# Lag tables built with half-scale squares and fewer complex products, in a newly ordered S4 convolution and GLU kernel

## The chip, the cores and the metric

The kernel runs on one core of one Trainium2 chip. The metric is the device time of one execution in microseconds (us); several executions are timed and their median is given. Engines are named as in the profile: PE is the matrix engine (PEld its weight loads), DVE the vector engine, ACT the scalar engine, POOL the GpSimd engine, SP the engine that issues most DMAs.

## The reference

The input is normalized by a layernorm, and two independent branches read the result; everything is bfloat16 at the edges.

```python
def _A_ref(u, A_re, A_im, B_re, B_im, C_re, C_im, log_dt, Dskip):   # u: [1, 2048, 512], A..C: [512, 128]
    dt = jnp.exp(log_dt)[:, None]
    logdA = dt * (A_re + 1j * A_im)
    dB = dt * (B_re + 1j * B_im)
    P = jnp.exp(logdA[:, :, None] * l[None, None, :])               # l = 0 .. 2047
    K = jnp.einsum("dn,dnl,dn->dl", C_re + 1j * C_im, P, dB).real    # one kernel of 2048 taps per channel
    ...                                                             # y = causal convolution of u with K, by rfft of length 4096
    return y + u * Dskip[None, None, :]

def _B_ref(x, w_gate, w_up, w_down):                                # 512 -> 1792 -> 512
    h = _sigmoid(x @ w_gate) * (x @ w_up)
    return h @ w_down

xn = _layernorm(x)
return x + _A_ref(xn, ...) + _B_ref(xn, ...)
```

## The kernel before

**Work of the two branches.** The GLU branch goes over four groups of 512 rows. For each group and each of 14 slices of the hidden width it runs four gate matmuls (line 1021), a sigmoid on ACT (1030), four up matmuls (1036) and a product on DVE (1051); then four sets of 14 down matmuls (1069). The product reads the up result either straight from its PSUM bank, or from an SBUF copy (`us_sb`) that ACT made (1047); the set `UEV` lists the units that take the copy.

The convolution branch never forms a long FFT. It transforms the input by matmuls with small constant matrices (691, through a DRAM scratch `z_scr`, then 891), multiplies it with the spectrum of K (products on DVE, lines 915 and 919), transforms back (932, through the scratch `v_scr`) and finishes with matmuls at line 989. The spectrum of K comes from matmuls with constant weights E (909), eight units for each half of the channels. The first 8 of the 16 products can run when half of the channels has its K, the last 8 need the other half.

**The lag tables.** K at the lag l is a sum over 128 modes of a power of a complex number. The power is split into two tables, G (16 steps of 16 lags, with C and dB in it) and H (41 base lags, listed in `LAG0`), and K is a matmul of the two (818). The tables are made in four parts of 128 channels each (loop variable `c`); all four use one buffer H, so a part may write H only when the matmuls of the part before have read it. Inside a part, new lags come from old ones in two ways. A *product* (`cmul`, called by `powers` for `n` lags at a time) multiplies by a constant power W: two wide DVE multiplies (729, 730), then a subtract and an add (734, 735). A *square* (`squares`) doubles the exponent: ACT squares real and imaginary parts in place (784), and DVE makes the real part by a subtract (789), the imaginary part by a product (790), and doubles it (791). The W come from a ladder of 11 repeated squarings in float32 (ACT 668, DVE 674 and 676, copies to bfloat16 on ACT 662).

**The start.** While weights arrive, DVE and ACT compute the layernorm statistics of each 128-row tile (`ON_ACT` lists the tiles that ACT takes), and the phase of the discretized A: DVE reduces it modulo one turn (619 to 621), ACT takes exponentials and sines (623 to 628), DVE combines them (635 to 637). Until real work is there, PE runs dummy matmuls on zeros (526).

**The order.** Nothing is scheduled at run time. All pieces of work are recorded as numbered operations with dependencies, and the table `ORDER` is the order in which they are written out; each engine executes its own instructions in just that order and waits on semaphores. Buffers are taken and given back in the same order.

Of the kernel before, what the change touches and what calls it, by code (L numbers as in the profile page):

```python
# [20 lines left out]
D = 512  # L21
# [33 lines left out]
LAG0 = (list(range(16)) + [256 + 2 * j for j in range(8)] + [512 + 4 * j for j in range(4)] + [768 + 4 * j for j in range(4)]  # L55
        + [1024, 1032, 1280, 1288, 1536, 1792, 1544, 1800, 2048])
# [104 lines left out]
def _build_E(S1, M2):  # L161

    E = np.zeros((NKT, 8, NGE, NU, 128))
    z = M2.reshape(NU, 2, 2, 32, 128)
    s1 = S1.reshape(32, NU, 2, 2)
    for l in range(L):
        h, i = _row(l)
        if h < 40 and (h < 32) == (l < 1024):
            E[h // 8, h % 8, i] += np.einsum("gpc,gpcf->gf", s1[l % 1024 // 32], z[:, :, :, l % 32, :])
    E = E.reshape(NKT, 128, NU, 128).transpose(1, 2, 0, 3)  # L170
    E[:, 1::2] = np.roll(E[:, 1::2], 64, axis=-1)
    return E

def _consts():
# [134 lines left out]
def kernel(  # L309
# [83 lines left out]
    for nm, sz in [("W1", 12 * KB), ("gc", 2 * KB), ("G", 16 * KB), ("H", 20992), ("tmp", 4 * KB), ("W0", 12 * KB),  # L393
                   ("xn", 16 * KB), ("lad", 16 * KB), ("kx", 8 * KB), ("zs", 4 * KB), ("pq", 2 * KB)]:
        OFF[nm] = o
        o += sz
    KQ = o
    W = [at(OFF["W%d" % p], [12, 2, DW]) for p in range(NP)]
    gc = at(OFF["gc"], [2, D])
    xn = at(OFF["xn"], [NT, D])  # L400

# [52 lines left out]
    for n in range(3):  # L454
# [3 lines left out]
        if n == 1:  # L458
            l_s1 = load("SP", s1[:], cten["S1"].ap(), 64 * KB)
# [680 lines left out]
```

## Time and profile before

| what | value |
|---|---|
| time before, median of 3 runs | 254.12 us (253.22 to 255.28) |
| the profiled execution's own time | 252.33 us |
| span of its instructions, first to last | 250.5 us |
| granted PE clock, mean | 0.986 |
| PE busy | 222.8 us (89%) |
| DVE busy | 202.0 us (81%) |
| ACT busy | 184.3 us (74%) |

The span is 1.8 us shorter than the execution's own time, and that execution is 1.8 us faster than the median of the timed runs. Matmuls are pipelined and the end of each is modelled, so the busy time of PE includes some waiting; how many matmuls of a kind start in a stretch says more. DVE instructions overlap at their ends as well: the distance from one start to the next is what an instruction costs there, and it is a little shorter than its duration.

### The profile page before, as it was taken

The numbers are of one execution on the slowest core, as the hardware profiler recorded it, in microseconds if no ns is written. First come the engines' busy times: TensorE is split into PE (matmuls) and PEld (weight loads), VectorE is DVE, ScalarE is ACT, GpSimd is POOL, SyncE is SP. The second block draws the span as 40 slices with busy tenths as digits, with TensorE's granted clock in tenths as the row PEclk, the third lists the DMA queues.
The fourth block names the chain that finished last, engine by engine and source line by source line (L and its number), as shares of the span: only waits on it lengthen the run. The fifth ranks groups of instructions, "written<-read, shape, count | busy, mean of one in ns | idle before, by whom it ended". The sixth has DMA issues, their size and how long they took to land.

```text
span 250.5 us, 5787 instructions
## 1 busy us (share of the span) xinstructions
PE 222.8 (89%) x2246; PEld 120.0 (48%) x2276; DVE 202.0 (81%) x445; ACT 184.3 (74%) x297; POOL 15.5 (6%) x34
## 2 busy tenths in 40 slices
PE   0799999999996799599999799979799999999994
PEld 0264444444432544246555556434565555544762
DVE  2999999999999999999999999999435244672652
ACT  5799999999998989358998698877446589740000
POOL 2202600010000000000000040000001010000000
PEclk9999999999999999979999799999999999999999
DMA  6999946305262585236737977734557698679263
GB/s 156 257 346 359 351 146 124 99 3 126 84 168 85 167 219 133 77 91 184 200 71 198 268 119 190 231 93 143 138 180 205 185 243 243 161 210 304 91 196 128
DMA packets 50861, 43.64 MB, mean 174 GB/s; under 512 B 12561, under 2 KB 44050, under 8 KB 50834
## 3 DMA queue, kind: packets, MB, share of 16 engines
q1 hardware_dynamic: 48738, 40.58, 55.8%
q0 software_dynamic: 864, 1.57, 3.9%
q10 hardware_dynamic: 1232, 1.11, 1.4%
q8 instruction: 18, 0.29, 0.5%
q14 instruction: 9, 0.07, 0.1%
HBM read 24.64 MB, written 12.06 MB: 147 GB/s over the span
## 4 chain that ended last, share of the span: by engine, by line
DVE 45%; PE 34%; ACT 11%; issue 6%; DMA 3%; DVEq 0%; ACTq 0%
PE bank L1021 8%; DVE big L729 8%; DVE big L730 8%; PE bank L1069 7%; DVE big L735 6%; DVE big L734 5%; PE bank L1036 5%; DVE hT_sb L1051 4%; PE pair L909 4%; DVE big L915 3%; ACT big L662 3%; DVE big L790 3%; PE pair L932 2%; DVE big L789 2%; DVE big L919 2%
## 5 line engine op out<-in xcount | busy, mean ns | idle before, releaser
L1021 PE MATMUL bank<-xnT,wg_sb 128*128 128x512 bf16 (+1 forms) x224 | 54.7, 368 | 3.3 <-ACT us_sb L1047 1.2
L1036 PE MATMUL bank<-xnT,wu_sb 128*128 128x512 bf16 x214 | 54.3, 379 | 3.2 <-DVE hT_sb L1051 1.2
L1069 PE MATMUL bank<-wd_sb,hT_sb 128*128 128x512 bf16 x217 | 52.0, 389 | 1.0 <-ACT glu_sb L1099 0.5
L1021 PEld LDWEIGHTS <-wg_sb 128*128 128x128 bf16 x236 | 22.3, 98 | 27.1 <-issue 5.9
L1030 ACT ACTIVATE hT_sb<-bank 128x512 bf16<-128x512 f32 x56 | 32.2, 598 | 4.1 <-PE bank L1021 4.0
L1069 PEld LDWEIGHTS <-hT_sb 128*128 128x128 bf16 x224 | 21.9, 100 | 27.4 <-issue 4.0
L1036 PEld LDWEIGHTS <-wu_sb 128*128 128x128 bf16 x224 | 20.8, 98 | 28.1 <-issue 5.5
L915 DVE TENSOR_TENSOR big<-big 128x2048 bf16<-128x2048 bf16 x16 | 19.5, 1220 | 14.1 <-DMA big<-big 7.2
L729 DVE TENSOR_TENSOR big<-big 128x512 bf16<-128x512 bf16 (+4 forms) x48 | 27.7, 577 | 1.0 <-ACT big L770 0.2
L730 DVE TENSOR_TENSOR big<-big 128x512 bf16<-128x512 bf16 (+4 forms) x48 | 27.5, 573 | 0.0
L1051 DVE TENSOR_TENSOR hT_sb<-hT_sb,bank 128x512 bf16<-128x512 bf16 x27 | 17.8, 682 | 7.0 <-ACT hT_sb L1030 4.6
L1047 ACT ACTIVATE us_sb<-bank 128x512 bf16<-128x512 f32 x29 | 17.1, 601 | 6.7 <-DVE hT_sb L1051 5.9
L734 DVE TENSOR_TENSOR big<-big 128x256 bf16<-128x256 bf16 (+4 forms) x48 | 20.2, 420 | 0.8
L911 ACT ACTIVATE big<-pair 128x1024 bf16<-128x1024 f32 x16 | 16.5, 1031 | 4.9 <-PE pair L909 3.6
L909 PE MATMUL pair<-big 128*128 128x256 bf16 x160 | 19.8, 273 | 0.3 <-DVE big L853 0.3
L735 DVE TENSOR_TENSOR big<-big 128x256 bf16<-128x256 bf16 (+4 forms) x48 | 20.0, 416 | 0.0
L896 ACT ACTIVATE big<-pair 128x1024 bf16<-128x1024 f32 x16 | 16.3, 1032 | 3.4 <-PE pair L891 3.4
L909 PEld LDWEIGHTS <-big 128*128 128x128 bf16 x160 | 15.3, 98 | 5.0 <-issue 1.5
L693 ACT ACTIVATE big<-pair 128x1024 bf16<-128x1024 f32 x16 | 16.3, 1023 | 1.6 <-PE pair L691 1.6
L936 ACT ACTIVATE big<-pair 128x1024 bf16<-128x1024 f32 x16 | 16.3, 1026 | 1.2 <-PE pair L932 0.4
L691 PE MATMUL pair<-big,s 128*128 128x512 bf16 x31 | 9.7, 394 | 7.9 <-DVE big L559 7.9
L784 ACT ACTIVATE big<-big 128x768 bf16<-128x768 bf16 (+2 forms) x16 | 11.0, 690 | 6.2 <-DVE big L735 6.1
(105 smaller groups left out, 285.2 us busy)
## 6 DMA issues: line engine op xcount, KB each, us to landing
big<-c_E SPq DMA_DIRECT2D x16, 320.0 KB, 3.6
z_scr<-big SPq DMA_DIRECT2D x16, 256.0 KB, 2.7
big<-z_scr SPq DMA_DIRECT2D x16, 256.0 KB, 3.7
big<-big SPq DMA_DIRECT2D x64, 64.0 KB, 3.1
v_scr<-big SPq DMA_DIRECT2D x16, 256.0 KB, 3.7
big<-v_scr SPq DMA_DIRECT2D x12, 256.0 KB, 4.6
big<-in_A_u_dram SPq DMA_DIRECT2D x4, 512.0 KB, 5.8
wu_sb<-in_B_w_up_dram SPq DMA_DIRECT2D x2, 896.0 KB, 6.7
```

Source lines behind the costliest of these rows:

```text
L729: V.tensor_tensor(out=ov, in0=lov, in1=mre, op=ALU.mult)
L730: V.tensor_tensor(out=wide(tb()), in0=lov, in1=mim, op=ALU.mult)
L734: V.tensor_tensor(out=outp[:, :, :, 0, :], in0=outp[:, :, :, 0, :], in1=tb()[:, :, :, 1, :], op=opr)
L735: V.tensor_tensor(out=outp[:, :, :, 1, :], in0=outp[:, :, :, 1, :], in1=tb()[:, :, :, 0, :], op=opi)
L909: T.matmul(two(sk)[:, o:o + DW], es()[:, g, kt, :], kT[p][:, kt, :], start=kt in (0, NKT - 1), stop=kt >= NKT - 2)
L915: V.tensor_tensor(out=pp().rearrange("p q h m -> p (q h) m"), in0=xx().rearrange("p q h m -> p (q h) m"), in1=kb()[:, 0:2 * DW].unsqueeze( ...
L1021: T.matmul(bank(sl)[:, c0:c1], w[:, kt, k * 128:(k + 1) * 128], xnT[:, grp, kt, c0:c1], start=(kt == 0), stop=(kt == KT - 1))
L1030: S.activation(out=hT_sb[:, hs.idx, k % 2, :], in_=bank(sl), func=ACT.Sigmoid)
L1036: T.matmul(bank(sl), wu_sb[:, kt, k * 128:(k + 1) * 128], xnT[:, grp, kt, :], start=(kt == 0), stop=(kt == KT - 1))
L1047: S.activation(out=us_sb[:, us.idx, :], in_=bank(sl), func=ACT.Identity)
L1051: V.tensor_tensor(out=h(), in0=h(), in1=us_sb[:, us.idx, :] if on else bank(sl), op=ALU.mult)
L1069: T.matmul(bank(po), hT_sb[:, hts[k // 2].idx, k % 2, jj * 128:(jj + 1) * 128], wd_sb[:, k, :], start=(k == 0), stop=k == FT - 1, **kw)
```

## The change

- **Squares at half scale.** ACT now squares with the scale 0.5^0.5 into a buffer of its own (`sq_sb`), and the doubling instruction on DVE is gone: what is stored is half of the true power. The constant weights E are multiplied by 2, or by 8 where a square of a square is meant, for the rows listed in `EXP`.
- **Lags in another order.** `LAG0` is rearranged, and a part of H is made by six products and five squares instead of eight products and four squares. The products of 1, 2 and 2 lags at `o0` = 33, 34 and 37 go, one of 4 lags at 33 comes, and a square of one lag (39 from 27) comes.
- **Phase steps on ACT.** The scaling by 1/(2 pi) with the rounding constant becomes one ACT instruction, the two DVE instructions after it do the rest, and 1 - 2 s^2 is one ACT instruction instead of one of DVE.
- **Other moves.** `ON_ACT` is tile 0 alone instead of tiles 1 and 3. `UEV` has 22 units instead of 29. The running sums of `f_pre` go from DVE to POOL. The constants s1, s2, sr and rr lie in space that other tiles use too, so the loads of s2 and sr and the clearing of rr wait for the last table matmul. `ORDER` is another list, and some of the planner's costs, which only served to find that list, are changed.

Lines of the changed kernel are 3 to 7 higher than those of the kernel before. The core of the diff:

```diff
+EXP = {6: 1, 10: 1, 12: 3, 14: 1, 19: 1, 21: 1, 22: 3, 23: 1, 27: 1, 29: 1, 31: 3, 30: 3, 37: 1, 38: 1, 39: 3}
...
-            E[h // 8, h % 8, i] += np.einsum("gpc,gpcf->gf", s1[l % 1024 // 32], z[:, :, :, l % 32, :])
+            E[h // 8, h % 8, i] += 2.0 ** EXP.get(h, 0) * np.einsum("gpc,gpcf->gf", s1[l % 1024 // 32], z[:, :, :, l % 32, :])
...
-UEV = (7, 14, 15, 16, 17, 18, 19, 21, 24, 25, 26, 28, 29, 30, 31, 32, 33, 34, 35, 36, 37, 38, 39, 40, 41, 42, 46, 49, 54)
-ON_ACT = (1, 3)
+UEV = (15, 19, 23, 24, 27, 28, 29, 30, 31, 32, 33, 34, 35, 36, 37, 38, 39, 40, 41, 42, 43, 44)
+ON_ACT = (0,)
 ORDER = [
-    0, 1, 29, 12, 4, 3, 30, 31, 39, 40, 2, 14, 19, 5, 10, 33, 32, 42, 34, 7, 17, 35, 41, 49, 50, 51, 43, 132, 25, 52, 15,
+    1, 0, 38, 28, 27, 37, 3, 4, 47, 2, 30, 29, 48, 50, 31, 49, 39, 52, 41, 51, 32, 14, 5, 7, 17, 10, 18, 6, 40, 34, 12, 42,
...
+    q2b = pl.add("ACT", 0.57, lambda: S.activation(out=pt_["rn"], in_=pt_["z_im"], func=ACT.Identity, scale=INV_2PI, bias=magic[:]), [q1], PR)
     def f_red():
-        V.tensor_scalar(out=pt_["w0"], in0=pt_["z_im"], scalar1=INV_2PI, scalar2=None, op0=ALU.mult)
-        V.tensor_scalar(out=pt_["rn"], in0=pt_["w0"], scalar1=MAGIC, scalar2=MAGIC, op0=ALU.add, op1=ALU.subtract)
-        V.tensor_tensor(out=pt_["w0"], in0=pt_["w0"], in1=pt_["rn"], op=ALU.subtract)
+        V.tensor_scalar(out=pt_["rn"], in0=pt_["rn"], scalar1=MAGIC, scalar2=None, op0=ALU.subtract)
+        V.scalar_tensor_tensor(out=pt_["w0"], in0=pt_["z_im"], scalar=INV_2PI, in1=pt_["rn"], op0=ALU.mult, op1=ALU.subtract)
...
+        S.activation(out=pt_["sh"], in_=pt_["sh"], func=ACT.Identity, scale=-2.0, bias=one[:])
...
-        V.tensor_scalar(out=pt_["sh"], in0=pt_["sh"], scalar1=-2.0, scalar2=1.0, op0=ALU.mult, op1=ALU.add)
...
-        def squares(o0, os, l0, nn, need):
+        def squares(o0, os, l0, ls, nn, need):
...
+            sl = _Slot("sq")
+            a = pl.add("ACT", 0.11 + 0.213 * nn, lambda: S.activation(out=sq().rearrange("p r k c h -> p r k (c h)"), in_=src.rearrange("p r k c h -> p r k (c h)"),
+                                                                      func=ACT.Square, scale=float(0.5 ** 0.5)),
+                       dep(need), PC - 0.5, acq=[sl])
             def f_q():
-                V.tensor_tensor(out=dst[:, :, :, 0, :], in0=dst[:, :, :, 0, :], in1=dst[:, :, :, 1, :], op=ALU.subtract)
+                V.tensor_tensor(out=dst[:, :, :, 0, :], in0=sq()[:, :, :, 0, :], in1=sq()[:, :, :, 1, :], op=ALU.subtract)
                 V.tensor_tensor(out=dst[:, :, :, 1, :], in0=src[:, :, :, 0, :], in1=src[:, :, :, 1, :], op=ALU.mult)
-                V.tensor_scalar(out=dst[:, :, :, 1, :], in0=dst[:, :, :, 1, :], scalar1=2.0, scalar2=None, op0=ALU.mult)
...
         powers(3, 1, 1, 1, 1, 1, [1])
...
-        squares(25, 1, 17, 3, ["17"])
-        powers(28, 1, 16, 2, 4, 9, [16, "17"])
-        powers(34, 1, 16, 4, 2, 10, [16, "17"])
-        squares(36, 2, 28, 2, ["28"])
-        powers(37, 2, 28, 2, 2, 10, ["28"])
-        powers(33, 1, 8, 1, 1, 10, [8])
+        squares(27, 2, 17, 1, 3, ["17"])
+        powers(24, 2, 16, 2, 4, 9, [16, "17"])
+        powers(33, 1, 16, 4, 4, 10, [16, "17", "24"])
+        squares(37, 1, 24, 2, 2, ["24"])
+        squares(39, 1, 27, 1, 1, ["27"])
...
+    l_sr = load("SP", sr, cten["SR"].ap(), 128 * KB, deps=table_free, pkt=1024)
+    l_s2 = load("SP", s2, cten["S2"].ap(), 64 * KB, deps=table_free)
+    m_rr = pl.add("POOL", 0.3, lambda: P.memset(rr, 0.0), table_free, 60)
```

The new order is seen best in the instructions. First, what DVE executes last in the fourth part of the tables. Before (729, 730, 734, 735 are a product, 789 to 791 a square; the last number is the output's shape):

```order
L729 TENSOR_TENSOR big<-big 128x64x8
L730 TENSOR_TENSOR big<-big 128x512
L729 TENSOR_TENSOR big<-big 128x64x2x4
L730 TENSOR_TENSOR big<-big 128x512
L734 TENSOR_TENSOR big<-big 128x64x2x2
L735 TENSOR_TENSOR big<-big 128x64x2x2
L789 TENSOR_TENSOR big<-big 128x64x2x2
L790 TENSOR_TENSOR big<-big 128x64x2x2
L791 TENSOR_SCALAR big<-big 128x64x2x2
```

The same place now, where 733, 734, 738, 739 are a product and 795, 796 a square:

```order
L733 TENSOR_TENSOR big<-big 128x64x16
L734 TENSOR_TENSOR big<-big 128x1024
L795 TENSOR_TENSOR big<-sq_sb 128x64x3x2
L796 TENSOR_TENSOR big<-big 128x64x3x2
L795 TENSOR_TENSOR big<-sq_sb 128x64x2x2
L796 TENSOR_TENSOR big<-big 128x64x2x2
L738 TENSOR_TENSOR big<-big 128x64x4x2
L739 TENSOR_TENSOR big<-big 128x64x4x2
L795 TENSOR_TENSOR big<-sq_sb 128x64x2
L796 TENSOR_TENSOR big<-big 128x64x2
```

Two products of two lags have become one of four, with two squares between its halves, and each square has two instructions in place of three.

Second, the start of PE. Before, it begins with the input transform of a first tile and 14 dummy matmuls (526), and only then come the transposes of the normalized tiles (570):

```order
L691 LDWEIGHTS s_70
L691 MATMUL pair_63<-big,s_70 128x512
...
L526 LDWEIGHTS glu_sb
L526 MATMUL bank_68<-glu_sb 128x512
...
L570 LDWEIGHTS big
L570 MATMUL pair_64<-ident,big 128x128
```

Now the transposes are the first instructions of PE, and the 14 dummies (529) stand behind 56 gate matmuls (1028), right ahead of the first up matmul (1043):

```order
L1028 LDWEIGHTS wg_sb
L1028 MATMUL bank_65<-xnT,wg_sb 128x512
L529 LDWEIGHTS glu_sb
L529 MATMUL bank_68<-glu_sb 128x512
...
L1043 LDWEIGHTS wu_sb
L1043 MATMUL bank_66<-xnT,wu_sb 128x512
```

So the dummies moved from a place where PE had nothing else to do to a place between real matmuls.

Third, ACT at the start, from the exponential of log_dt to the first copy of transposed input (575). Before:

```order
L611 ACTIVATE big<-big 128x512
L693 ACTIVATE big<-pair_63 128x1024
L623 ACTIVATE big<-big 128x512
L626 ACT_TABLE_LOAD
L626 ACTIVATE big<-big 128x512
L627 ACTIVATE big<-big 128x512
L628 ACTIVATE big<-big 128x512
L575 ACTIVATE xnT<-pair_64 128x4x256
```

Now, with the two added steps at 621 and 633:

```order
L614 ACTIVATE big<-big 128x512
L621 ACTIVATE big<-big,magic 128x512
L627 ACTIVATE big<-big 128x512
L630 ACT_TABLE_LOAD
L630 ACTIVATE big<-big 128x512
L631 ACTIVATE big<-big 128x512
L632 ACTIVATE big<-big 128x512
L633 ACTIVATE big<-big,one 128x512
L578 ACTIVATE xnT<-pair_63 128x4x256
```

The evacuation of a transformed tile (693) has left this place, and two short steps of the phase have come into it, one of them right ahead of the first copy of transposed input.

More of the change, by code (lines that the diff above doesn't have):

```diff
@@ L352 @@
     ident = const.tile([128, 128], BF, name="ident")
-    s1 = const.tile([128, 2, 128], BF, name="s1")
-    s2 = const.tile([128, 2, 128], BF, name="s2")
     dskr = const.tile([1, D], BF, name="dskr")
@@ L357 @@
     rz = const.tile([128, KT, 8], BF, name="rz")
-    rr = const.tile([128, D], BF, name="rr")
-    sr = const.tile([128, 4, 128], BF, name="sr")
+    sq_sb = const.tile([128, 2, NPR * 12], BF, name="sq_sb")
     wg_sb = const.tile([128, KT, F], BF, name="wg_sb")
@@ L458 @@
         if n == 1:
-            l_s1 = load("SP", s1[:], cten["S1"].ap(), 64 * KB)
+            l_s1 = load("SP", s1, cten["S1"].ap(), 64 * KB)
         if n:
@@ L499, in fw_ @@
                 V.tensor_copy(out=q["m_f"], in_=q["m_b"])
-            o_v = pl.add("DVE", 0.37, fv_, deps, prio)
+            o_v = pl.add("DVE", 0.8 if t1 - t0 > 1 else 0.37, fv_, deps, prio)
             o_w = pl.add("DVE", 0.22, fw_, deps, prio)
@@ L516 @@
     half = const.tile([128, NT], BF, name="half")
+    magic = const.tile([128, 1], F32, name="magic")
+    one = const.tile([128, 1], F32, name="one")
     P.memset(half[:], 0.5)
+    P.memset(magic[:], MAGIC)
+    P.memset(one[:], 1.0)
     P.memset(glu_sb[:, 0, :], 0.0)
     P.memset(rz[:], 0.0)
-    P.memset(rr[:], 0.0)
     wsl = _Slot("po")
@@ L628, in f_sin @@
         S.activation(out=pt_["sh"], in_=pt_["sh"], func=ACT.Square)
-    q5 = pl.add("ACT", 1.6, f_sin, [q3, q4], PR, tab="sin")
+        S.activation(out=pt_["sh"], in_=pt_["sh"], func=ACT.Identity, scale=-2.0, bias=one[:])
+    q5 = pl.add("ACT", 2.15, f_sin, [q3, q4], PR, tab="sin")
     lad0 = OFF["lad"]
@@ L634, in f_w0 @@
     def f_w0():
[L635 removed]
         V.tensor_tensor(out=wt[0][:, 0, :], in0=pt_["rr"], in1=pt_["sh"], op=ALU.mult)
         V.tensor_tensor(out=wt[0][:, 1, :], in0=pt_["rr"], in1=pt_["sn"], op=ALU.mult)
[L638 removed]
+    cur_op = pl.add("DVE", 1.25, f_w0, [q5], PR)
     def f_g():
@@ L642, in f_g @@
         tt(perm(pt_["db_im"]), raw("B", 1), perm(dtb), ALU.mult)
-    qb = pl.add("DVE", 2.0, f_g, [o_dt] + pt_op["B"], PR + 2)
+    qb = pl.add("DVE", 1.21, f_g, [o_dt] + pt_op["B"], PR + 2)
     def f_g2():
@@ L648, in f_g2 @@
         tt(gc[:, 0, :], pt_["t1"], pt_["t2"], ALU.subtract)
-    qc1 = pl.add("DVE", 1.9, f_g2, [qb] + pt_op["C"], PR + 2)
+    qc1 = pl.add("DVE", 2.02, f_g2, [qb] + pt_op["C"], PR + 2)
     def f_g3():
@@ L701, in f_pre @@
     def f_pre():
-        V.tensor_copy(out=pre[:, :, 0], in_=xnT[:, 0, :, 0])
+        P.tensor_copy(out=pre[:, :, 0], in_=xnT[:, 0, :, 0])
         for t in range(1, 4):
-            V.tensor_tensor(out=pre[:, :, t], in0=pre[:, :, t - 1], in1=xnT[:, 0, :, 128 * t], op=ALU.add)
-        V.tensor_copy(out=pre2[:, :, 0], in_=xnT[:, 0, :, 64])
-        V.tensor_tensor(out=pre2[:, :, 1], in0=pre2[:, :, 0], in1=xnT[:, 0, :, 192], op=ALU.add)
-    o_pre = pl.add("DVE", 1.0, f_pre, xnT_ready[0], 47)
+            P.tensor_tensor(out=pre[:, :, t], in0=pre[:, :, t - 1], in1=xnT[:, 0, :, 128 * t], op=ALU.add)
+        P.tensor_copy(out=pre2[:, :, 0], in_=xnT[:, 0, :, 64])
+        P.tensor_tensor(out=pre2[:, :, 1], in0=pre2[:, :, 0], in1=xnT[:, 0, :, 192], op=ALU.add)
+    o_pre = pl.add("POOL", 2.0, f_pre, xnT_ready[0], 47)
     kq = at(KQ, [NHP, 16])
@@ L736, in cmul @@
         a = pl.add("DVE", 0.14 + 0.27 * n, f_a, deps, prio, acq=[sl])
-        return pl.add("DVE", {1: 0.37, 2: 0.45, 3: 0.62, 4: 0.70}.get(n, 0.15 + 0.134 * n), f_b, [a], prio - 0.1, rel=[sl])
+        return pl.add("DVE", {1: 0.37, 2: 0.48, 4: 0.73, 7: 1.19}.get(n, 0.15 + 0.134 * n), f_b, [a], prio - 0.1, rel=[sl])
     kgen = {}
@@ L792, in squares @@
-            h_ops[str(o0)] = pl.add("DVE", 0.18 + 0.185 * nn, f_q, [a], PC - 0.5)
+            h_ops[str(o0)] = pl.add("DVE", 0.22 + 0.134 * nn, f_q, [a] + hdep, PC - 0.5, rel=[sl])
         powers(3, 1, 1, 1, 1, 1, [1])
-        squares(6, 1, 3, 1, ["3"])
+        squares(6, 1, 3, 1, 1, ["3"])
         powers(5, 2, 1, 2, 2, 2, [1, "3"])
         powers(9, 2, 1, 2, 4, 3, [1, "3", "5"])
-        squares(10, 2, 5, 3, ["5", "6"])
+        squares(10, 2, 5, 1, 3, ["5", "6"])
         powers(17, 1, 2, 2, 7, 8, [2, 4, 8, "6", "10"])
-        squares(25, 1, 17, 3, ["17"])
@@ L961, in f_rz @@
         V.tensor_tensor(out=rz[:, :, 5:8:2], in0=rf[:, :, 2:4], in1=rf[:, :, 4:6], op=ALU.add)
-    o_rz = pl.add("DVE", 0.66, f_rz, [mk2, o_pre], 60, rel=[slk])
+    o_rz = pl.add("DVE", 1.15, f_rz, [mk2, o_pre], 60, rel=[slk])
     slr = _Slot("s")
@@ L968 @@
     o_rt = pl.add("PE", 0.32, f_rt, [o_rz], 60, acq=[slr])
-    o_rz = pl.add("ACT", 0.48, lambda slr=slr: S.activation(out=rr[0:8, :], in_=bank(slr)[0:8, :], func=ACT.Identity), [o_rt, l_sr], 60, rel=[slr])
+    o_rz = pl.add("ACT", 0.48, lambda slr=slr: S.activation(out=rr[0:8, :], in_=bank(slr)[0:8, :], func=ACT.Identity), [o_rt, l_sr, m_rr], 60, rel=[slr])
     vp_op = []
```

23 lines of the change are left out of this document (11 added, 12 removed), and 80 rows, old and new, of the table ORDER.

## The prediction

> **What bounds the kernel now.** The page's busy times come first, then DVE's in 40 slices of the span, then the chain of work that ended last.
>
> ```profile
> PE 222.8 (89%) x2246; PEld 120.0 (48%) x2276; DVE 202.0 (81%) x445; ACT 184.3 (74%) x297; POOL 15.5 (6%) x34
> DVE  2999999999999999999999999999435244672652
> DVE 45%; PE 34%; ACT 11%; issue 6%; DMA 3%; DVEq 0%; ACTq 0%
> ```
>
> No engine is the bound of the whole: DVE is full for the first 70% of the span, and the chain runs over DVE 45%. After that DVE has room and PE is full. So I cut the span where the matmuls of the four lag tables start (line 818). Three of these starts, with the wait ahead of each, in PE's timeline:
>
> ```profile
> 84.29 2.76 PE L818 MATMUL pair<-big 128*32 128x82 bf16 x128 [1.52 <-DVE big L734]
> ...
> 141.02 2.69 PE L818 MATMUL pair<-big 128*32 128x82 bf16 x128 [1.55 <-DVE big L734]
> ...
> 176.41 0.25 PE L818 MATMUL pair<-big 128*32 128x82 bf16 x4 [0.91 <-DVE big L789]
> ```
>
> and ask for the busy times between these points (before the comma the stretch and its length, then busy time and instruction count of PE, its loads, DVE, ACT, POOL, and the granted clock):
>
> ```profile
> 14.80:84.30 69.50, 63.99 (x299) 29.40 (x304) 67.53 (x153) 68.22 (x116) 6.82 (x12) 1.00 0.54 160
> 84.30:111.80 27.50, 24.47 (x296) 11.81 (x298) 26.78 (x68) 18.96 (x35) 0.35 (x2) 0.94 0.53 147
> 111.80:141.00 29.20, 26.93 (x403) 16.41 (x405) 28.65 (x63) 26.16 (x42) 0.36 (x2) 1.00 0.63 173
> 141.00:176.40 35.40, 32.10 (x462) 18.00 (x469) 34.82 (x78) 27.84 (x45) 3.02 (x5) 0.95 0.64 165
> 176.40:250.50 74.10, 68.63 (x759) 41.19 (x770) 34.46 (x57) 32.80 (x43) 1.73 (x2) 1.00 0.67 193
> ```
>
> The first of these four table matmuls waits 1.52 us for DVE, the third 1.55, the last 0.91, and between the first and the last DVE is idle for 27.5 - 26.78 + 29.2 - 28.65 + 35.4 - 34.82 = 1.85 us of 92.1. So **DVE sets when the last table starts, 176.4**. The 74.1 us behind it are PE's: 68.6 busy, DVE at half load. The time follows from two numbers: when the last table starts, and what PE has left then.
>
> What PE has left I count in the two orders, matmul by matmul, with the distance of their starts from the chain:
>
> ```profile
> 186.92 3.02 PE bank L1069 x14
> ...
> 211.91 1.09 PE pair L909 x10
> ```
>
> A matmul of 512 columns costs 3.02/14 = 0.216 us, one of 256 columns (909) 0.109. Behind the last table there are 182 of 512 columns before and 186 now, two of them dummies behind everything; all other kinds are equal. The tail grows by 2 x 0.216 = **+0.4 us**.
>
> **The change part by part: DVE ahead of the last table.** I count distances from one start to the next. Products and squares of the third part:
>
> ```profile
> 120.89 0.63 DVE L734 TENSOR_TENSOR big<-big 128x512 bf16<-128x512 bf16 x1
> ...
> 121.96 1.21 DVE L915 TENSOR_TENSOR big<-big 128x2048 bf16<-128x2048 bf16 x1
> ...
> 131.04 0.69 DVE L730 TENSOR_TENSOR big<-big 128x1024 bf16<-128x1024 bf16 x1
> 131.65 1.22 DVE L915 TENSOR_TENSOR big<-big 128x2048 bf16<-128x2048 bf16 x1
> ...
> 134.05 0.44 DVE L734 TENSOR_TENSOR big<-big 128x512 bf16<-128x512 bf16 x1
> ...
> 134.75 0.28 DVE L729 TENSOR_TENSOR big<-big 128x256 bf16<-128x256 bf16 x1
> ...
> 135.62 0.42 DVE L729 TENSOR_TENSOR big<-big 128x512 bf16<-128x512 bf16 x1
> 135.95 0.42 DVE L730 TENSOR_TENSOR big<-big 128x512 bf16<-128x512 bf16 x1
> 136.41 0.39 DVE L734 TENSOR_TENSOR big<-big 128x256 bf16<-128x256 bf16 x1
> ...
> 137.01 1.21 DVE L915 TENSOR_TENSOR big<-big 128x2048 bf16<-128x2048 bf16 x1
> 138.14 0.37 DVE L789 TENSOR_TENSOR big<-big 128x384 bf16<-128x384 bf16 x1
> 138.55 0.40 DVE L790 TENSOR_TENSOR big<-big 128x384 bf16<-128x384 bf16 x1
> 138.98 0.29 DVE L791 TENSOR_SCALAR big<-big 128x384 bf16<-128x384 bf16 x1
> 139.17 0.39 DVE L789 TENSOR_TENSOR big<-big 128x256 bf16<-128x256 bf16 x1
> ...
> 140.20 0.29 DVE L729 TENSOR_TENSOR big<-big 128x256 bf16<-128x256 bf16 x1
> ...
> 140.61 0.27 DVE L734 TENSOR_TENSOR big<-big 128x128 bf16<-128x128 bf16 x1
> 140.79 0.27 DVE L735 TENSOR_TENSOR big<-big 128x128 bf16<-128x128 bf16 x1
> 140.96 0.68 DVE L919 TENSOR_TENSOR big<-big 128x1024 bf16<-128x1024 bf16 x1
> ```
>
> *Products.* One of one lag costs 140.96 - 140.20 = 0.76 us. One of two costs 137.01 - 135.62 = 1.39, of which 0.12 is a wait between its halves (136.41 starts 0.04 behind the end of 135.95, not 0.08 ahead of it); I take 1.3. One of four costs 2 x 0.61 for its wide half (131.04 to 131.65) and, for the narrow half, 0.70 (134.05 to 134.75) or 1.07 (120.89 to 121.96): 1.9 to 2.3, and I take 2.1, since both layouts occur. A part loses 0.76 + 2 x 1.3 and gains 2.1: -1.26 (bounds -1.0 and -1.6).
>
> *Squares.* The doubling is 139.17 - 138.98 = 0.19, four times a part: -0.76. Before, the product of a square overwrites what the subtract reads, and the doubling reads what the product wrote. The rows show it: 138.55 starts 0.04 after its forerunner's end, and 138.98 0.03 after, where unbound neighbours start 0.09 and 0.10 ahead of that end (140.79, 140.96). With `sq_sb` neither dependence is left. That is about 0.1 to 0.12 each, 0.2 a square, -0.8 a part; bounds 0 and -0.9. The new square of one lag has two instructions like 140.61, 2 x 0.18 = +0.36 (with waits +0.6). Squares: -1.2 a part, bounds -0.2 and -1.3. Together -2.46 a part, **-9.8 us** in four (bounds -4.6 and -11.6). The Trainium skill speaks against a piece of this: "VectorE: DVE Perf Modes", section "The DRAIN you can't avoid", says that waits between vector instructions add nothing to the flush that follows each of them anyway, so one should count instructions and not semaphores. By it the four parts give 3.2 us less. The rows above differ, with a start after the end in one case and ahead of it in the other.
>
> *Products of the GLU from PSUM.* Of the 42 units that stand ahead of the last table, 17 read PSUM before and 23 now.
>
> ```profile
> L1051 DVE TENSOR_TENSOR hT_sb<-hT_sb,bank 128x512 bf16<-128x512 bf16 x27 | 17.8, 682 | 7.0 <-ACT hT_sb L1030 4.6 <-PE bank L1036 2.3
> L1051 DVE TENSOR_TENSOR hT_sb<-hT_sb,us_sb 128x512 bf16<-128x512 bf16 x29 | 11.8, 417 | 0.0
> L547 DVE BATCH_NORM_STATS2 stats<-big 128x6 f32<-128x512 bf16 x14 | 9.4, 670 | 3.8 <-DMA big<-in_A_u_dram 3.8
> L483 POOL CAST ln_v_b<-mv 128x4 bf16<-128x4 f32 x3 | 0.9, 308 | 13.6 <-DVE mv L548 13.6
> L1047 ACT ACTIVATE us_sb<-bank 128x512 bf16<-128x512 f32 x29 | 17.1, 601 | 6.7 <-DVE hT_sb L1051 5.9 <-PE bank L1036 0.8
> ...
> 9.68 0.42 DVE L619 TENSOR_SCALAR big<-big 128x512 f32<-128x512 f32 x1
> ...
> 10.59 0.69 DVE L621 TENSOR_TENSOR big<-big 128x512 f32<-128x512 f32 x1
> 11.20 0.41 DVE L559 TENSOR_SCALAR big<-big,ln_m_f,ln_ri_f 128x512 bf16<-128x512 bf16 x1
> ```
>
> Each costs 0.682 - 0.417 = 0.265 more: **+1.6**. One more tile has its statistics on DVE: 0.67, less some 0.1 of overlap and 0.1 of small steps, **+0.5**. The phase loses 1.52 of three steps (9.68 to 11.20) and pays 0.42 + 0.61, and loses a step like the first, 0.42: **-0.9**. ACT pays two steps of 0.6 for it; but it also loses one tile's statistics and the evacuation at 693 at that place, so that the first gate matmul, now at 14.8, stays within 13.4 to 15.4; I take 14.1. `f_pre` stood behind the last table, so it gives DVE nothing ahead of it; on POOL, six steps like L483's 308 ns stand in front of the waits of that group, 13.6 us, which cover them. The loads of s2 and sr wait for the last table in SP's queue, behind loads of `v_scr` that wait for the same: nothing.
>
> Sum for DVE: -9.8 + 1.6 + 0.5 - 0.9 = **-8.6 us** (bounds -3.4 and -10.4). Going row by row through both orders with these distances, it falls as +0.8, -4, 0 and -5 on the four stretches: the first has fewer savings than bank reads and statistics, so no table comes earlier before the second.
>
> **What comes in its place.** PE must bring its own work to each table. From the first gate matmul to the first table there are 278 matmuls of 512 columns before and 302 now: the 14 dummies, 6 input transforms and 4 more gates and 4 more ups, less 4 dummies. That is +5.2 us; the start may give back 0.7. Before, PE needed 278 x 0.216 + 24 x 0.109 = 62.7 us of the 69.5, and lost 6.8 to waits. Now it needs 67.9: the first table cannot start before 82.0 without any wait, and starts at 88.8 with the old ones. DVE is ready at 84.3 + 0.8 = 85.1. I take the middle of 85.1 and 88.8 or a little more, 87.2. DVE cannot make this up, because H is free for the second part only when the first table's matmuls have read it. From there DVE needs 92.1 - 1.85 - 9.4 = 80.9 and PE 76.1 by the same count; so DVE is still the longer, with PE at 94%. Something like it has been reached: in the row of 111.80 above, PE was busy for 92% with DVE full too. With 2.9 us for the idle of DVE, more than the 1.85 because PE is tighter, the last table starts at 87.2 + 80.9 + 2.9 = **171.0**, 5.4 earlier. Given back: 3.2 of 8.6.
>
> ACT does not stop this: ahead of the last table it loses 6 copies of 0.6 (1047) and a tile's statistics (1.6), and gains two phase steps and four squares (4 x 0.43), about -2.3.
>
> So the span becomes 250.5 - 5.4 + 0.4 = 245.5, the own time of this execution 252.33 - 5.0 = 247.3. That execution was 1.8 us faster than the median shown; on the scale of the median it is 254.12 - 5.0 = 249.1.
>
> **The rivals.** *All of DVE's saving arrives.* PE's waits at the first table shrink with DVE's load, the last table starts at 176.4 - 8.6 = 167.8, and the median is 254.12 - 8.6 + 0.4 = 245.9. For it: PE's waits there mostly name DVE or ACT. Against it: PE would need 82.0 of the 85.1.
>
> *PE becomes the bound, and the kernel is slower.* The place is the start of PE, the dummies behind 56 gate matmuls, and the price is waits that stay as they were. Before, PE had, by the same count, 140.9 us of work from the first gate to the last table in 161.6: 20.7 of waits. Now it has 12 matmuls more, 143.5. With the same 20.7 from 14.1 the last table starts at 178.3. There is a second price: without the early dummies the transposes and first gates meet a slow PE.
>
> ```profile
> 8.88 4.36 PE bank L526 x14
> ```
>
> Fourteen dummies took 4.36 us at the start against 3.02 warm, 1.3 lost. With it the last table starts at 179.6 and the median is 254.12 + 3.2 + 0.4 = 257.7. The point from which it decides: PE's waits ahead of the last table must stay above 17.5 us. The Trainium skill, "TensorE: Matmul & The Clock Gate", section "Part 1: The HAM clock gate", has the array at half its clock until about 3.4 us of activity have passed; the rows agree, and by it the price is at most 1.7 us instead of 1.3. Against the rival: most of these waits were DVE's.
>
> *PE takes part of the place.* Half of that: the last table at 174.5, the median at 252.6, within 1% of before. *The squares save only their doubling*, because the waits inside them cost nothing or move to the next pair: 3.2 us less, the median at 252.3, also no change. The rule on the flush, above, would end here.
>
> **How the numbers follow.** A measurement of this kernel tells about 1%, 2.5 us, from no change. Chances: the forecast 0.47, all of the saving 0.19 (both faster), PE takes part 0.17 and squares save only the doubling 0.07 (both the same), PE the bound 0.10 (slower). That makes 0.66, 0.24, 0.10. The range goes from 254.12 - 10.4 + 0.4 = 244.1, DVE's saving in full and at its better bound, to 256.0, PE's waits all but unchanged.
>
> **What would show it.** Right, if DVE's busy time falls by 8 to 10 us with 16 doublings gone and 12 small products replaced by 4 of four lags, squares of two instructions start ahead of their forerunner's end, the first table starts at 86 to 88, the last near 171, and 74.5 us follow it. Wrong, if the first table comes after 90 with DVE idle behind it, if PE's waits ahead of the last table name ACT, or if the tail behind the last table grows by more than 2 us.

## The result: 244.5 us, more than the forecast gained

The changed kernel took 244.47 us (244.02 to 245.01, 4 runs) against 253.67 us before (253.18 to 255.28), a ratio of 0.9628, 95% interval [0.9577, 0.9678]. Measured once more (a_again) it took 244.69 us (4 runs), ratio 0.9692 [0.9632, 0.9752]; before's medians in the later series lie between 252.74 and 253.38. The variants below are set against this 244.69. One of the ten runs of a_three (1259.64 us) and two of the four of a_pool (251.55 and 252.79) stand far off the others of their kernel, and the ratios leave these three out. So the change saves 8.4 to 9.2 us. The forecast was 249.1: the direction and the engine were right, the size was little more than half, and the time is close to the first rival, "all of DVE's saving arrives" (245.9). In the trace the last table starts at 168.96, between the forecast (171.0) and that rival (167.8).

The page of the changed kernel, with the busy times and the chain of work that ended last:

```profile
PE 218.4 (90%) x2248; PEld 120.6 (50%) x2276; DVE 193.2 (80%) x397; ACT 180.8 (75%) x292; POOL 17.1 (7%) x42
PE 35%; DVE 30%; ACT 23%; DMA 7%; issue 3%; SPq 1%; DVEq 0%; ACTq 0%
```

DVE's busy time falls from 202.0 to 193.2, and the chain runs over DVE for 30% of the span instead of 45%. PE's timeline, at the starts of the four lag tables (line 822 now), with the wait ahead of each at the row's end:

```profile
86.67 2.69 PE L822 MATMUL pair<-big 128*32 128x82 bf16 x128
107.29 2.78 PE L822 MATMUL pair<-big 128*32 128x82 bf16 x128 [1.21 <-DVE big L795]
138.33 2.68 PE L822 MATMUL pair<-big 128*32 128x82 bf16 x128 [0.25 <-DVE big L796]
168.96 2.75 PE L822 MATMUL pair<-big 128*32 128x82 bf16 x128 [0.44 <-DVE big L795]
```

The first table starts 2.4 us later than before, the last 7.4 us earlier (168.96 against 176.41). The stretches between these starts, with the same columns as in the prediction (the first one begins here at 13.5, though the first gate matmul starts at 14.89, no earlier than before):

```profile
13.50:86.70 73.20, 70.83 (x329) 32.71 (x337) 69.96 (x148) 70.92 (x118) 8.20 (x18) 1.00 0.59 179
86.70:107.30 20.60, 19.02 (x285) 9.87 (x286) 20.29 (x48) 16.59 (x32) 1.22 (x3) 1.00 0.49 122
107.30:138.30 31.00, 29.00 (x431) 17.83 (x436) 30.72 (x65) 25.59 (x44) 2.09 (x4) 1.00 0.74 191
138.30:169.00 30.70, 29.27 (x439) 16.97 (x444) 30.53 (x63) 27.97 (x46) 0.35 (x2) 1.00 0.54 154
169.00:242.70 73.70, 68.69 (x764) 41.58 (x774) 33.28 (x50) 31.99 (x42) 2.27 (x3) 1.00 0.70 201
```

Behind the first table DVE is idle for only 20.6 - 20.29 + 31.0 - 30.72 + 30.7 - 30.53 = 0.76 us of 82.3, less than before (1.85 of 92.1), though PE is busier. The stretch behind the last table is 73.7 us long, 0.4 less than before.

What became of the squares shows in DVE's timeline in the third part, the place of the rows from 138.14 in the prediction:

```profile
136.01 0.50 DVE L795 TENSOR_TENSOR big<-sq_sb 128x384 bf16<-128x384 bf16 x1
136.34 0.52 DVE L796 TENSOR_TENSOR big<-big 128x384 bf16<-128x384 bf16 x1
136.69 0.45 DVE L738 TENSOR_TENSOR big<-big 128x512 bf16<-128x512 bf16 x1
...
137.38 0.32 DVE L795 TENSOR_TENSOR big<-sq_sb 128x256 bf16<-128x256 bf16 x1
137.58 0.38 DVE L796 TENSOR_TENSOR big<-big 128x256 bf16<-128x256 bf16 x1
137.89 0.26 DVE L795 TENSOR_TENSOR big<-sq_sb 128x128 bf16<-128x128 bf16 x1
138.02 0.26 DVE L796 TENSOR_TENSOR big<-big 128x128 bf16<-128x128 bf16 x1
138.21 0.31 DVE L738 TENSOR_TENSOR big<-big 128x256 bf16<-128x256 bf16 x1
```

The square of three lags costs 136.69 - 136.01 = 0.68 us where it cost 1.03, that of two 0.51 where it cost 1.03. The two kernels' squares of three lags do not lie alike in H: the subtract at 136.01 is 0.50 long, the one at 138.14 before was 0.37. With the layout of before the new square costs less still, 0.57 (b_sq below). The product (796) starts 0.17 ahead of the end of its subtract (136.34 against 136.51), where before it started 0.04 behind.

### The profile page after: what moved, and what is told of

Same layout as the page of the kernel before. It is cut to its first block, busy times and chain, and to the rows that moved or that the text cites. A ratio compares the mean times of both kernels' runs of the same rounds, so it can differ in the third digit from the quotient of the medians.

```text
span 242.7 us, 5745 instructions
## 1 busy us (share of the span) xinstructions
PE 218.4 (90%) x2248; PEld 120.6 (50%) x2276; DVE 193.2 (80%) x397; ACT 180.8 (75%) x292; POOL 17.1 (7%) x42
## 4 chain that ended last, share of the span: by engine, by line
PE 35%; DVE 30%; ACT 23%; DMA 7%; issue 3%; SPq 1%; DVEq 0%; ACTq 0%
PE bank L1076 10%; PE bank L1028 6%; DVE big L733 5%; DVE big L734 5%; PE pair L916 5%; ACT big L666 4%; ACT big L672 4%; DVE big L739 4%; PE bank L1043 4%; DVE big L738 4%; ACT hT_sb L1037 3%; DVE hT_sb L1058 3%; ACT big L697 3%; PE pair L939 3%; ACT big L557 3%
## 5 line engine op out<-in xcount | busy, mean ns | idle before, releaser
L1043 PE MATMUL bank<-xnT,wu_sb 128*128 128x512 bf16 x214 | 53.3, 379 | 2.0 <-DVE hT_sb L1058 1.1
L1076 PE MATMUL bank<-wd_sb,hT_sb 128*128 128x512 bf16 x216 | 50.3, 379 | 0.6 <-issue 0.2
L1028 PEld LDWEIGHTS <-wg_sb 128*128 128x128 bf16 x236 | 23.1, 100 | 27.4 <-issue 4.1
L1076 PEld LDWEIGHTS <-hT_sb 128*128 128x128 bf16 x224 | 21.4, 98 | 25.1 <-issue 0.4
L733 DVE TENSOR_TENSOR big<-big 128x1024 bf16<-128x1024 bf16 (+4 forms) x40 | 25.9, 647 | 0.9
L734 DVE TENSOR_TENSOR big<-big 128x1024 bf16<-128x1024 bf16 (+4 forms) x40 | 25.8, 644 | 0.0
L1058 DVE TENSOR_TENSOR hT_sb<-hT_sb,bank 128x512 bf16<-128x512 bf16 x34 | 22.4, 681 | 3.7 <-PE bank L1043 2.1
L738 DVE TENSOR_TENSOR big<-big 128x512 bf16<-128x512 bf16 (+4 forms) x40 | 18.8, 469 | 0.6
L739 DVE TENSOR_TENSOR big<-big 128x512 bf16<-128x512 bf16 (+4 forms) x40 | 18.5, 463 | 0.0
L790 ACT ACTIVATE sq_sb<-big 128x256 bf16<-128x256 bf16 (+2 forms) x20 | 12.7, 632 | 4.5 <-DVE big L796 3.1
L1054 ACT ACTIVATE us_sb<-bank 128x512 bf16<-128x512 f32 x22 | 13.0, 598 | 1.0 <-DVE hT_sb L1058 0.9
L666 ACT ACTIVATE big<-big 128x512 bf16<-128x512 f32 x24 | 13.8, 628 | 0.0
```

The source lines that it names most:

```text
L666: S.activation(out=W[p][:, k], in_=cur[:, :, DW * p:DW * p + DW], func=ACT.Identity)
L733: V.tensor_tensor(out=ov, in0=lov, in1=mre, op=ALU.mult)
L734: V.tensor_tensor(out=wide(tb()), in0=lov, in1=mim, op=ALU.mult)
L738: V.tensor_tensor(out=outp[:, :, :, 0, :], in0=outp[:, :, :, 0, :], in1=tb()[:, :, :, 1, :], op=opr)
L739: V.tensor_tensor(out=outp[:, :, :, 1, :], in0=outp[:, :, :, 1, :], in1=tb()[:, :, :, 0, :], op=opi)
L1028: T.matmul(bank(sl)[:, c0:c1], w[:, kt, k * 128:(k + 1) * 128], xnT[:, grp, kt, c0:c1], start=(kt == 0), stop=(kt == KT - 1))
```

## The experiments

Two theories of where the forecast went wrong were put against each other: A, that DVE's work goes into the time one for one, and B, that PE takes a part back, as forecast. Theory C is that the change gained a part of its time by doing away with falls of PE's granted clock.

**The third instruction of a square** (a_three). The changed kernel with

```diff
                 V.tensor_tensor(out=dst[:, :, :, 1, :], in0=src[:, :, :, 0, :], in1=src[:, :, :, 1, :], op=ALU.mult)
+                V.tensor_scalar(out=dst[:, :, :, 1, :], in0=dst[:, :, :, 1, :], scalar1=1.0, scalar2=None, op0=ALU.mult)
```

> The changed kernel, with a third DVE instruction put back into each of its 20 squares: the product's result times 1.0, in place, at the position of the former doubling. Theory A (DVE's own work sets when each lag table starts, one for one): by the distances 0.13 to 0.25 of the former doubling the instructions cost 3.6 us, and up to 5.6 if each also waits 0.1 for the product before it; time 248 to 250. Theory B (PE is so tight after the change that it takes back a part of what DVE gains or loses): half, 1.8 to 2.8 us, 246.3 to 247.3.

It took 252.29 us, ratio to before 0.9952 [0.9926, 0.9977]: 7.6 us more for 20 small instructions, more than either theory gave and nothing that PE took back. Its DVE timeline in the third part, and its last table:

```profile
140.30 0.53 DVE L796 TENSOR_TENSOR big<-big 128x384 bf16<-128x384 bf16 x1
140.86 0.34 DVE L797 TENSOR_SCALAR big<-big 128x384 bf16<-128x384 bf16 x1
141.11 0.45 DVE L738 TENSOR_TENSOR big<-big 128x512 bf16<-128x512 bf16 x1
...
175.43 3.00 PE L823 MATMUL pair<-big 128*32 128x82 bf16 x128 [1.15 <-DVE big L795]
```

From the product to the next instruction it is 0.81 us here and 0.35 above (136.34 to 136.69): the third instruction costs 0.46, not its distance of 0.25, because it also starts only behind the end of the product that it reads (140.86 against 140.83). The last table starts 6.5 us later. The rest of the 7.6 lies behind it.

**The wait inside a square** (a_inplace). ACT's squares go into the rows of H again, with the number of instructions unchanged:

```diff
-            a = ... S.activation(out=sq()..., in_=src..., func=ACT.Square, scale=float(0.5 ** 0.5))
+            a = ... S.activation(out=dst..., in_=src..., func=ACT.Square, scale=float(0.5 ** 0.5))
-                V.tensor_tensor(out=dst[:, :, :, 0, :], in0=sq()[:, :, :, 0, :], in1=sq()[:, :, :, 1, :], op=ALU.subtract)
+                V.tensor_tensor(out=dst[:, :, :, 0, :], in0=dst[:, :, :, 0, :], in1=dst[:, :, :, 1, :], op=ALU.subtract)
```

> The changed kernel, its ACT squares written into the destination rows of H again, not into sq_sb; the number of instructions is unchanged, but the product of each square overwrites what its subtract has just read. If such a wait inside a square costs time (theory A, 20 squares with 0.1 to 0.2 us each), 246.5 to 248.5. If waits between DVE instructions cost nothing, 244.5 plus or minus 0.5.

It took 248.08 us, ratio 0.9794 [0.9751, 0.9837], 3.4 us more than the changed kernel. Its DVE timeline and last table:

```profile
136.71 0.50 DVE L795 TENSOR_TENSOR big<-big 128x384 bf16<-128x384 bf16 x1
137.25 0.51 DVE L796 TENSOR_TENSOR big<-big 128x384 bf16<-128x384 bf16 x1
...
170.99 2.95 PE L822 MATMUL pair<-big 128*32 128x82 bf16 x128 [0.80 <-DVE big L795]
```

The product starts 0.54 behind its subtract instead of 0.33; with 256 elements it is 0.36 instead of 0.20, with 128 it is 0.31 instead of 0.13. So a wait inside a pair of neighbours on DVE costs 0.15 to 0.21 us here, 20 times. In the traces the last table starts 2.0 us later. The first table started 0.7 earlier in this execution (85.95), and from the first to the last table it is 85.0 us instead of 82.3: 2.7 more, which is what the 15 squares between them pay at 0.18. The rule of the Trainium skill that the prediction weighed ("VectorE: DVE Perf Modes", "The DRAIN you can't avoid": a semaphore costs nothing extra) does not hold for this pair: 397 DVE instructions in both kernels, their medians 3.4 us apart. Another sentence of that section, that an instruction which is not held back starts earlier, agrees with these rows.

**Both** (a_old), the two edits above together.

> The changed kernel with squares as before in both respects: in place, and with a third DVE instruction (times 1.0). If the two costs add up: 6.5 + 2.0 us more until the last table, span 251 to 253 and time 253 to 256, so that nothing of the gain is left. If the wait inside the square and the third instruction hide each other: 251 to 252.5.

255.3 us, ratio 1.0105 [1.0037, 1.0172]. The two costs add up (7.6 + 3.4 = 11.0, measured 10.6), and all of the gain is gone: the new lags, the order, the copies and the phase with squares of the old kind (20 of them instead of 16) are no faster than before.

**The squares alone, from the other side** (b_two, b_sq). The kernel before, first only without its 16 doublings, then with squares just as in the change. To make room for `sq_sb`, b_sq also has s1, s2, sr and rr in space of other tiles, and the loads of s2 and sr and the clearing of rr come later in its order, as in the change:

```diff
+            E[h // 8, h % 8, i] += 2.0 ** EXP.get(h, 0) * np.einsum(...)     # EXP for before's lags
+            ... func=ACT.Square, scale=float(0.5 ** 0.5))                    # b_sq: out=sq()
-                V.tensor_scalar(out=dst[:, :, :, 1, :], in0=dst[:, :, :, 1, :], scalar1=2.0, scalar2=None, op0=ALU.mult)
```

> The kernel before with squares at half scale: the doubling instruction on DVE is gone, 16 in all, the spectrum weights take the factor; squares stay in place, and lag order and order of work are those of before. Theory A: the doublings' distances sum to 0.76 a part, 3.0 us, and up to 4.6 if the wait ahead of each goes too; time 249 to 250.7. Theory B, where PE's waits and clock hold the tables: half of that or less, 251.4 to 252.2.

> The kernel before with the new squares alone: half scale, two DVE instructions, ACT's squares in sq_sb (room for it comes from the late constants, as in the change); lag order, eight products, copies, phase and the order of the work stay as before. If the squares carry the gain (16 x 0.29 us for the doublings, 16 x 0.145 for the waits inside, 7 us of DVE time): 246 to 247.5. If the new lag order, the product of four and the new order of work carry a good part: 249 to 250, no better than without the doublings alone.

b_two: 249.94 us, ratio 0.9867 [0.9824, 0.991], 3.2 us for the 16 doublings, as theory A had it. b_sq: 245.96 us, ratio 0.9708 [0.9638, 0.9778]. The page of b_sq, its squares of three and two lags in the third part (subtract at 751, product at 752), and the start of its last table (779):

```profile
PE 221.6 (90%) x2246; PEld 119.5 (49%) x2276; DVE 195.1 (80%) x429; ACT 183.6 (75%) x297; POOL 15.6 (6%) x34
...
133.85 0.39 DVE L751 TENSOR_TENSOR big<-sq_sb 128x384 bf16<-128x384 bf16 x1
134.12 0.39 DVE L752 TENSOR_TENSOR big<-big 128x384 bf16<-128x384 bf16 x1
134.42 0.38 DVE L751 TENSOR_TENSOR big<-sq_sb 128x256 bf16<-128x256 bf16 x1
...
170.62 2.69 PE L779 MATMUL pair<-big 128*32 128x82 bf16 x122 [0.30 <-DVE big L751]
```

DVE's busy time falls by 6.9 (202.0 to 195.1) and the time by 6.8 (252.74 to 245.96 within that series). So the squares alone bring about four fifths of what the whole change brings. What is left for the new lags, the order, the copies and the phase is 1 to 2 us, and the intervals of b_sq and of the change overlap, so that this rest is not separately shown.

**One product of four or two of two** (a_split). Each of the four instructions of the product at o0 = 33 is issued as two, for two lags each:

```diff
+                for q in (0, 2):   # halves of the four lags
+                    V.tensor_tensor(out=w2(o2), in0=w2(l2), in1=r2, op=ALU.mult)
+                    V.tensor_tensor(out=wide(t2), in0=w2(l2), in1=i2, op=ALU.mult)
```

> The changed kernel with its product of four lags at o0 = 33 executed as two products of two lags (8 DVE instructions instead of 4, in the same place, the same data). Theory A: 2 x 1.3 for 1.9 us in each of four parts, 2.8 us more, 247 to 248. Theory B (PE gives back half): 245.5 to 246.3.

245.6 us, ratio 0.9705 [0.9659, 0.975], 0.9 more than the changed kernel beside it, with 1.1 us more of DVE's busy time (194.3). The time lies in theory B's range, but not because PE took something back: on DVE itself the edit costs only 1.2 us, by the distances of the rows that it replaces. A product of two costs 1.12 in this run, not the 1.3 that the prediction took from one of 1.39 with a wait in it, and the product of four 1.96, not 2.1.

**PE's dummies** (a_nodum):

```diff
-    keep_warm(14, -10)
+    keep_warm(0, -10)
```

> The changed kernel without the 14 dummy matmuls behind its first 56 gate matmuls. Theory B (PE's own work holds the first table at 86.7): 3.0 us of PE work go, the first table starts 1.5 to 3 us earlier and the time is 241.5 to 243. Theory A (DVE brings its operands at 86.2 in any case, and the dummies lie where PE would wait for the up weights): first table at 86.2 to 87.2, time 244 to 245.

245.45 us, ratio 0.969 [0.9638, 0.9742], no gain. Its PE timeline behind the first gates, and at the first table:

```profile
28.43 1.02 PE L1028 MATMUL bank<-xnT,wg_sb 128*128 128x512 bf16 x4 [1.41 <-ACT hT_sb L1037]
...
86.03 2.67 PE L822 MATMUL pair<-big 128*32 128x82 bf16 x128
```

Where the dummies stood, PE waits 1.41 us for ACT's sigmoid. With 3.0 us less to do it comes to the first table 0.6 earlier (86.03 for 86.67), and two executions of the changed kernel itself differ by 0.2 there (86.43 in a_again). Beyond these 0.6 us PE's work does not hold the first table.

**The clock** (b_fill). The kernel before, with 11 dummies in front of the wait of 2.74 us and 6 in front of that of 1.55:

```diff
+    fill(11)    # in ORDER ahead of the transform (891) that started at 106.33
+    fill(6)     # in ORDER ahead of the third table
```

> The kernel before with 11 and 6 dummy matmuls written into the two places where PE waited 2.74 us (at 103.6) and 1.55 us (at 139.5) and the granted clock fell to half behind the wait. Theory C (the change gained a part of its time by doing away with these falls of the clock): the 14 down matmuls at 106.7 take 3.0 instead of 4.9, the time falls by 2 to 3 us, to 250 to 251. Theory A (DVE sets the tables, and PE has the slack to be slow there): 252.5 to 253.5, with the clock at 1.0.

253.92 us, ratio 1.0017 [0.9979, 1.0056]. PE's timeline at the first of the two places with the page's granted clock, before and in b_fill, where the down matmuls are at line 1028:

```profile
PEclk9999999999999999979999799999999999999999
106.33 0.41 PE L891 MATMUL pair<-big,m 64*64 64x256 bf16 x8 [2.74 <-DVE big L853]
106.68 4.88 PE L1069 MATMUL bank<-wd_sb,hT_sb 128*128 128x512 bf16 x14
```

```profile
PEclk9999999999999999999999999999999999999999
109.00 3.19 PE L1028 MATMUL bank<-wd_sb,hT_sb 128*128 128x512 bf16 x14
```

The 14 down matmuls behind the wait take 3.19 instead of 4.88 us, no slice of the clock is below 9 any more, and the kernel is no faster; from the first table to the last it takes 92.6 us, before 92.1. In before's profile the falls of the clock lay in PE's slack. Theory C is out.

**ACT** (a_sbuf4, a_act4). Four more units with copies, then four copies that nobody reads:

```diff
-UEV = (15, 19, 23, 24, ...
+UEV = (7, 16, 18, 21, 15, 19, 23, 24, ...                                  # a_sbuf4
+        if k in (3, 5, 7, 9):                                              # a_act4
+            S.activation(out=glu_sb[:, 7, :]..., in_=cur[:, :, 0:DW], func=ACT.Identity)
```

> The changed kernel with four more units (7, 16, 18, 21, all ahead of the first table) that read an SBUF copy made by ACT: 4 x 0.265 = 1.06 us less on DVE, 2.4 us more on ACT. If DVE alone sets the first table: 243.5 to 244. If ACT, 70.9 of 73.2 us busy there, is as full: 245.5 to 247.

> The changed kernel with four more ACT instructions in the ladder of W powers, each a copy of 128x512 to an unused row (4 x 0.57 = 2.3 us, all before 65 us); nothing reads them, and no slot or wait of another engine changes. If ACT holds the first table: it starts 2 to 2.5 us later, 88.5 to 89, and the time is 246.5 to 247. If PE or DVE holds it, ACT's waits take the 2.3 us in: 86.4 to 87, 244.5 to 245.

a_sbuf4 took 248.58 us, ratio 0.9826 [0.9762, 0.989], although DVE has less to do (192.7 us busy for 193.2), and more than either expectation gave; why it is more stays open. a_act4 took 246.64 us, ratio 0.9723 [0.9665, 0.978], 2.0 more than the changed kernel. Their first tables in PE's timeline, first of a_sbuf4, then of a_act4:

```profile
90.22 2.71 PE L822 MATMUL pair<-big 128*32 128x82 bf16 x128
```

```profile
88.70 2.71 PE L824 MATMUL pair<-big 128*32 128x82 bf16 x128
```

2.3 us of ACT's time alone move the first table by 2.0 (86.67 to 88.70), and the later tables by as much; the ratios' intervals of a_act4 and of the change overlap, so it is the trace that tells. The chain of the changed kernel says the same for that stretch; these are its pieces behind the first gates:

```profile
18.09 1.08 ACT hT_sb L1037 x2
19.17 1.03 ACT big L666 x2
20.21 0.97 ACT hT_sb L1037 x2
21.18 0.91 ACT big L697
```

It stays on ACT until 65.7 with few breaks, and goes over to DVE from there. The last square of the first part ends on DVE at 86.22 in the changed kernel and at 88.25 in a_act4, and the table follows 0.45 later in both. So ACT holds the first table, through DVE behind it.

**Phase steps** (a_phase), all on DVE again, as in before's lines 619 to 621.

> The changed kernel with all phase steps on DVE again: three DVE steps in place of ACT's one and DVE's two, and the last one ahead of the ladder. Theory A: DVE's 0.9 us more at the start move every table, 245.3 to 246. If ACT holds the start (its two steps stand ahead of the first copy of transposed input): 243.5 to 244.5.

244.87 us, ratio 0.9666 [0.9606, 0.9725], the same as the change. 0.8 us more of DVE's busy time and 1.3 less of ACT's leave the first table where it was (86.60 for 86.67), at a place where both are full.

**Work for POOL** (a_pool, a_poolcast). Subtracts of the larger squares, or four casts of the ladder, on POOL:

```diff
+                (P if o0 in (10, 27, 37) else V).tensor_tensor(out=dst[:, :, :, 0, :], ..., op=ALU.subtract)   # a_pool
+            if p == 1 and k in (5, 7, 9, 11):                                                                  # a_poolcast
+                P.tensor_copy(out=W[p][:, k], in_=cur[:, :, DW * p:DW * p + DW])
```

> The changed kernel with the subtract of three squares a part (o0 = 10, 27, 37) on POOL instead of DVE: 0.86 us a part less for DVE, 3.4 us in all. Theory A without a price on POOL: 241 to 242. If POOL is slow at it (no row here has such an instruction) and the next product waits for it: 246 to 252.

> The changed kernel with four of the ladder's 24 casts (second half of the channels, 128x512, needed late) on POOL instead of ACT, 2.3 us less for ACT ahead of the first table. If ACT holds the first table and POOL disturbs nothing: 85 or earlier, 242.5 to 243.5. If DVE instructions beside POOL's grow, as the products beside POOL's subtracts did (0.69 to 1.26): 244 to 246, no gain.

a_pool took 245.58 and 246.17 us in the two runs that its ratio takes, ratio 0.9712 [0.9621, 0.9803]; a_poolcast 245.84 us, ratio 0.9704 [0.9654, 0.9754]. Neither is faster than the change. In a_poolcast ACT is busy 1.6 us less and DVE 1.1 more, and the first table starts at 87.43, no earlier: taking work from ACT was not shown to bring the table forward, only adding work to delay it. In a_pool, POOL's timeline first, then DVE's:

```profile
101.59 0.83 POOL L795 TENSOR_TENSOR big<-sq_sb 128x384 bf16<-128x384 bf16 x1 [5.92 <-ACT sq_sb L790]
102.60 0.84 POOL L795 TENSOR_TENSOR big<-sq_sb 128x256 bf16<-128x256 bf16 x1 [0.18 <-ACT sq_sb L790]
```

```profile
99.11 0.69 DVE L733 TENSOR_TENSOR big<-big 128x1024 bf16<-128x1024 bf16 x1
...
101.71 1.26 DVE L733 TENSOR_TENSOR big<-big 128x1024 bf16<-128x1024 bf16 x1
102.89 1.10 DVE L734 TENSOR_TENSOR big<-big 128x1024 bf16<-128x1024 bf16 x1
```

The same multiply of a DVE product takes 0.69 alone and 1.26 where a subtract on POOL had started just before it. Where DVE's two multiplies were already running, from 68.69 in this run, each took 0.70, and it was POOL's subtract, from 69.16, that took 1.53 us instead of 0.83. The Trainium skill ("SBUF — State Buffer", section "SBUF: two separate sides") tells of a port pair that the two engines can only hold in turn; these rows agree. DVE lost 12 subtracts and its busy time still grew, from 193.2 to 194.7. No kernel tried here is faster than the change.

## Why the prediction was too small

**DVE's sum was right.** The distances of all DVE rows ahead of the last table, without the idle time, sum to 171.5 us before and 162.4 now, 9.1 less; forecast 8.6. Inside it two errors nearly cancel. Squares: 16.7 to 10.7, -5.9, forecast -4.8; the wait between two bound neighbours was taken as 0.1 to 0.12 and is 0.15 to 0.21 (a_inplace), because the freed product of three lags starts 0.17 ahead of its forerunner's end, not 0.09 or 0.10 as the rows of 128x128 did. Products: 83.1 to 79.2, -3.9, forecast -5.0; a product of two was priced too high (a_split). Products of the GLU: 18.6 to 20.3, +1.7, forecast +1.6. Behind the first table the forecast had DVE's work at -4, 0 and -5 on the three stretches; its busy time there changed by -6.5, +2.1 and -4.3, so the sum held and the shares did not.

**The step that failed is "What comes in its place".** It gave back 3.2 of 8.6 us: 2.1 at the first table (87.2 for the 85.1 at which DVE would be ready) and 1.1 as 2.9 us of DVE idle time in place of 1.85, "because PE is tighter". The second term is the one that came out wrong. The idle time is 0.76, and DVE ran from the first table to the last in 82.3 us instead of 83.8, though its own work there was 0.6 more than forecast. PE, busy for 94% of these stretches, cost DVE nothing. With the 0.5 by which the first table came earlier than forecast, that makes the 2.0 us between 171.0 and 168.96. The first term came out near the mark, 86.7 for 87.2, by luck: three microseconds of PE work less move the first table by 0.6 (a_nodum), 2.3 us of ACT work move it by 2.0 (a_act4), and the 0.7 that the start was to give back did not come. "ACT does not stop this" was the wrong sentence: it counted ACT's sum up to the last table, which falls, and not ACT in the first stretch, where it is full (70.92 of 73.2).

**The tail** grew by 0.4 in the forecast and shrank by 0.4. In before's PE timeline the last table halts once it has begun:

```profile
177.06 2.51 PE L818 MATMUL pair<-big 128*32 128x82 bf16 x118 [0.40 <-DVE big L791]
```

Four of its matmuls started at 176.41, the others only at 177.06, behind the doubling (791) of the last square. This half microsecond was counted behind 176.4 as PE's own work; it was DVE's, and went with the saving. The other 0.2 to 0.3 of the 0.8 us between forecast and trace stays open.

**The scale.** Last table 2.0 and tail 0.8 make the 2.8 us by which the traces differ from the forecast (span 242.7 for 245.5). The rest of the 4.6 is that before's profiled execution, 252.33, was shorter than all 4 of its timed runs in the result, while that of the change, 244.69, lies among its own: trace to trace 7.6 us, median to median 9.2.

**Right** were: the engine that sets the tables behind the first, the doublings gone with DVE's busy time down by 8 to 10 (8.8), squares of two instructions that overlap, and that the loads of the late constants and `f_pre` cost nothing that shows (no wait of PE's behind the last table names a DMA or POOL). The rival on PE (257.7) fell with a_nodum, that on squares saving only their doubling with a_inplace.

## What to carry to other kernels

Price a DVE instruction that reads or overwrites what its neighbour just touched by the distance between bound neighbours, not by its own length: here a third instruction whose own distance was 0.25 us cost 0.46, and taking away the buffer for a square's inputs cost 3.4 us, beside 7.6 for 20 instructions more. Before a saving is given back to another engine, ask stretch by stretch whether that engine's waits would vanish; a busy share of 94% is no stall. Two engines that are both full in one stretch (ACT and DVE ahead of the first table) are told apart by adding time to one of them; moving work from one to the other showed nothing here.

## What the runs showed of the hardware

A wait between neighbours on DVE has a price of its own, about 0.2 us for 128x384 elements (0.54 against 0.33 from start to start). DVE multiplies of 128x1024 elements grew from 0.69 to 1.26 us where a subtract on POOL had started before them, so that work moved to POOL was not free for DVE; where DVE had started first, the subtract took longer instead (1.53 us, against 0.83). And a fall of the granted clock that made 14 matmuls take 4.88 us instead of 3.19 cost this kernel nothing, since PE had that much slack there.
